# Another written order for the steady blocks, the opening and the last two blocks of a fused attention and feed-forward kernel, without the hold on batch 3's loads

## The chip, the cores and the metric

The kernel runs on one core of one Trainium2 chip. The metric is the device time of one execution in microseconds; the time before is the median of three runs.

## The reference

```
k_proj = einsum('ks,bhsd->bhkd', E, k);  v_proj = einsum('ks,bhsd->bhkd', F, v)
scores = matmul(q, k_proj^T) / sqrt(64)
attn = exp(scores - max);  attn = attn / (sum(attn) + 1e-09)
x = matmul(attn, v_proj)  -> transposed and reshaped to (8192, 512)
h = x @ w_in;  g = h * (1 / (1 + exp(-1.702 * h)));  out = g @ w_out
```

q, k and v are (8, 8, 1024, 64): 8 batches, 8 heads, 1024 positions, 64 wide. E and F are (64, 1024), w_in is (512, 2048), w_out is (2048, 512). All are float32 in DRAM; the kernel computes in bf16 with float32 sums.

## The kernel before, in words

**Blocks.** The 8192 rows are taken in 16 blocks of 512, numbered j = 0 to 15; batch b holds blocks 2b and 2b + 1. TensorE (PE) does all products; every product lands in one of eight PSUM banks, and VectorE (DVE) or ScalarE (ACT) must read it from there before the bank can be written anew.

**Batch work** (once for two blocks): `ld` loads k and v of the next batch, `lq` loads its q (both on GpSimd's, POOL's, DMA queue), `pj` projects k and v (16 matmuls of 128 rows by 64 columns), `kb` copies the projected k out of PSUM, `kd` and `qd` transpose k and q by DMA on SyncE's (SP's) queue, `vq` copies the projected v. `hold` is a copy of one element on POOL that waits for a transfer to land, so that what is queued behind it on POOL, `ld` and `lq`, starts no earlier. For j = 4 it reads the broadcast of block 3 (the tile rbc), for other blocks the transposed k and q of the batch (lines 723 to 726).

**Attention of a block:** `sc.0`, `sc.1` (scores: eight matmuls each of 64 rows by 32 columns, "small tiles"), `ex` (four exponentials on ACT, which need another activation table than the gelu; `gt` loads the gelu's table back), `su` (the sums of the exponentials, small tiles), `den` (copies of them), `ga` (a DMA that spreads them over 128 partitions), `rc` (reciprocal on DVE), `sr` (a DMA to DRAM), `sb` (two DMAs that broadcast them to all partitions as rbc), `va.0`, `va.1` (attention times v, small tiles) and `mv` (four products with rbc on DVE that give xT, the input of the feed-forward part). For block 3 the DMAs ga, sr and sb go on POOL's queue, otherwise on SP's. In blocks 0 to 2 the tokens are normalised in another way (`tk`, `tm`, `xr`, `xc`).

**Feed-forward part.** Both products are done with seven instead of eight half-size products (Winograd's form of Strassen's scheme). First product: for each of four column groups n the steps `un.P1` to `un.P7` (four matmuls of 128 by 128 by 256 each) add up in three accumulators A, B and G in three banks; `un.c1`, `c2`, `c3` copy, `d1`, `d2` add, and `g11`, `g12`, `g21`, `g22` are the gelus on ACT that write gT. `xs` and `gs` are the sums of inputs that the scheme needs (DVE). Second product: `F1` to `F7`, each in two halves of eight such matmuls; `Fc1` to `Fc3` copy, `Fd1`, `Fd2` add, `Fo0`, `Fo1` copy to the output tile, `st` stores. The temporaries of block 2's first groups lie in the buffer that rbc uses (line 622).

**Order.** Nothing is scheduled by a planner at run time: each engine executes its instructions in the order in which they are written, and the order is three lists of words. `OPEN` (line 480) is run once, from F1.0 of block 1 to block 5; `STEPS` (line 465) is run for j = 5 to 13, where `u2.c1` means block j, `va.0+1` block j + 1 and `st0-1` block j - 1, and the batch words are left out for odd j (lines 834 to 839); `END` (line 524) is run last, for blocks 13 to 15. In `OPEN` and `END` a word is step@block, `!` moves a copy to the other engine, and the numbers behind the colon are the PSUM banks; in `STEPS` the banks come from `BANK` (line 476) and the engine of a copy from `ON_ACT`. A step that writes a bank waits until the last reader of what stood there is done. Text below writes sc.0@2 for the step sc.0 of block 2.

In the list before, PE's small-tile steps of a steady block stand in four places: `va.0`, then `va.1` and (even j) `pj`, then `sc.0 sc.1`, then `su`, with full 128 by 128 matmuls between them.

Of the kernel before, what the change touches and what calls it, by code (L numbers as in the profile page):

```python
# [18 lines left out]
def kernel(ctx, tc, q, k, v, E, F,  # L19
                                                     moe_w_in, moe_w_out, out):  # L20
    nc = tc.nc
    B, H, S, D = q.shape
# [3 lines left out]
    J = S // P  # L26
# [430 lines left out]
    def ffn2_ops(j):  # L457
# [23 lines left out]
        F1.0@1:0 F1.1@1 sc.0@2:1,2 Fc1@1!:3 sc.1@2:4,5 ex.0.1@2 ex.0.0@2 F5.0@1:6 ex.1.1@2 F2.0@1 F6.0@1
        tk.0.1@2:7 tm.0.1@2 tk.1.0@2:2 tk.0.0@2:1 tm.0.0@2 F6.1@1 ex.1.0@2 tk.1.1@2:5 tm.1.0@2 Fc2@1! F2.1@1
        tk.2.1@2:4 tm.1.1@2 xr.0.0@2:7 xr.0.1@2:1 Fo0@1 xr.1.0@2:2 F5.1@1 tm.2.1@2 xr.1.1@2:5 xc.1.0@2
        tk.3.1@2:0 xc.1.1@2 tk.3.0@2:4 xc.0.1@2 F7.0@1 xc.0.0@2 sc.1@3:2,5 sc.0@3:1,7 ex.1.0@3 tm.3.0@2 ex.1.1@3
        F7.1@1 Fc3@1! ex.0.0@3 xr.3.0@2:4 tk.2.0@2:2 Fd1@1 tm.3.1@2 ex.0.1@3 F3.0@1 su@3:5,1 xc.3.0@2 den.0@3
        den.1@3 tm.2.0@2 xs.0@2 xr.2.1@2:7 u0.P1@2:0 u0.c1@2:5 xc.2.1@2 F4.0@1 xr.3.1@2:4 F4.1@1 xc.3.1@2
        xr.2.0@2:1 qd@4 xs.1@2 xc.2.0@2 u1.P1@2:2 Fo1@1 u0.P5@2:7 u0.P6@2 u1.c1@2:3 u1.P6@2 u0.P2@2 u0.c3@2!
        u1.P5@2:4 u1.c2@2 xs.2@2 u0.c2@2! u1.c3@2! u0.P3@2 pj@4:1 u0.d2@2 gt@2 u0.g11@2 u1.P3@2 u1.P7@2 ga@3
        kb@4! u0.P7@2 rc@3 u1.d2@2 u2.P1@2:7 u1.d1@2 u1.P2@2 u0.d1@2 u3.P5@2:0 xs.3@2 u0.g12@2 u1.g12@2
        u2.P5@2:4 u1.g22@2 u0.g22@2 u0.P4@2 vq.1@4 u1.P4@2 F3.1@1 gs1.0@2 u2.c3@2! Fd2@1 u1.g11@2 sr@3 kd@4  # L490
        u0.g21@2 u2.c1@2:2 u3.P1@2:5 u3.c3@2 u1.g21@2 st0@1 st1@1 u2.P2@2 u2.P6@2 u2.P3@2 u3.c1@2:6 u3.P2@2
        u3.P6@2 u2.g11@2 sc.0@4:3,7 vq.0@4 u3.g11@2 u2.c2@2! sc.0@5:1,5 u2.P7@2 u3.c2@2 u2.d2@2 ex.0.1@4
        ex.0.1@5 u2.d1@2 u3.P3@2 u3.P7@2 sb@3 u2.P4@2 ex.0.0@5 u3.d2@2 va.0@3:4,7 ex.0.0@4 u3.d1@2 sc.1@5:0,5
        mv.0.0@3 ex.1.1@5 ex.1.0@5 u3.P4@2 sc.1@4:1,3 mv.0.1@3 va.1@3:4,5 F1.0@2:7 ex.1.1@4 su@5:0,3 ex.1.0@4
        mv.1.0@3 su@4:4,1 mv.1.1@3 F1.1@2 xs.0@3 den.1@4 den.0@4 den.0@5 xs.2@3 u1.P1@3:5 xs.1@3 gt@2 u2.g21@2
        u0.P5@3:1 u3.g21@2 Fc1@2:2 u2.g12@2 ga@4 u0.P1@3:4 den.1@5 u1.P5@3:6 u0.c1@3:0 F2.0@2 u0.P2@3 u0.P6@3
        u3.g22@2 u1.c3@3! F2.1@2 u1.c1@3:3 u1.P6@3 u3.g12@2 u1.P2@3 u2.g22@2 gs2.0@2 gs3.0@2 u1.P3@3 gs1.1@2
        u1.c2@3 u0.c3@3 gs2.1@2 u0.g11@3 u3.P1@3:4 rc@4 u1.d2@3 u1.P7@3 F6.0@2 u0.P3@3 F6.1@2 F5.0@2:6 Fc2@2
        Fo0@2 F5.1@2 u2.P1@3:7 u0.c2@3 gs3.1@2 u1.g11@3 F7.0@2 sr@4 xs.3@3 F7.1@2 Fc3@2! u0.d2@3 u3.c1@3:5 Fd1@2
        ga@5 u3.P6@3 u0.P7@3 u1.g12@3 u1.d1@3 u3.P2@3 F4.0@2 F4.1@2 u0.d1@3 gs4.1@2 u2.c1@3:1 u2.P6@3 sb@4  # L500
        u0.P4@3 u3.c2@3 Fo1@2 u0.g12@3 gs4.0@2 u1.g22@3 u0.g21@3 u3.P5@3:2 F3.0@2 u2.c2@3! u3.c3@3! u0.g22@3
        rc@5 gs3.0@3 hold@4 ld@4 u3.P7@3 F3.1@2 Fd2@2 u3.P3@3 u1.P4@3 u1.g21@3 u3.d2@3 u2.P2@3 va.0@4:0,6 u2.g11@3
        pj@6:2 gs1.0@3 u3.g11@3 sr@5 u3.d1@3 u3.g22@3 vq.0@6 va.1@4:3,7 u2.P5@3:4 u2.P7@3 u2.c3@3 kb@6! u3.P4@3
        mv.0.1@4 lq@4 mv.1.1@4 mv.0.0@4 xs.0@4 F1.0@3:6 u2.d1@3 vq.1@6! u2.P3@3 u0.P5@4:7 u3.g21@3 mv.1.0@4
# [42 lines left out]
    def step(name, j, banks=None, swap=False):  # L547
# [324 lines left out]
```

## Time and profile before

| | us |
|---|---|
| median of 3 runs | 474.62 (474.2 to 475.11) |
| the profiled execution | 474.2, of which its span 472.4 |
| PE busy | 462.0 |
| VectorE busy | 331.8 |
| ScalarE busy | 319.1 |
| GpSimd busy | 92.7 |
| block 6 (with pj) / block 7 (without), from list start to list start | 28.30 / 26.46 |

The span is the time from the program's first instruction to its last in the profiled execution. Busy time is the union of an engine's instructions; matmuls are pipelined, so PE's rate is read from the distance between starts, not from durations. In the profile's lines "L639" is line 639 of the kernel (the P steps), L585 the F steps, L274 the small tiles of sc and va, L701 su and L184 the projection. A chain of waits is followed back from the last instruction, at each step to what released it.

| DMA of the profile | queue | issues | median us to landing |
|---|---|---|---|
| k of a batch | POOL | 7 | 11.3 |
| v of a batch | POOL | 7 | 14.8 |
| q, an eighth of a batch | POOL | 48 | 16.2 |
| rbc from DRAM (sb) | SP | 24 | 7.3 |
| stores | SP | 31 | 2.7 |

### The profile page before, as it was taken

What the parts mean: (1) busy time and instruction counts of PE and PEld (TensorE: products, weight loads), DVE (VectorE), ACT (ScalarE), POOL (GpSimd) and SP (SyncE); (2) the same over time, 40 slices, a digit from 0 to 9 for tenths busy, and PEclk for the clock granted to TensorE, in tenths of its full rate; (3) what the DMA queues carried; (4) which work ended last, traced back from release to release, by engine and by line L of the source; (5) the groups of instructions that cost most, each with busy time, mean ns of one, the idle gap of its engine ahead of it and who ended that gap; (6) DMA issues with size and microseconds to landing.
All of it is one profiled execution on the core that took longest, in us unless ns stands there. A gap on an engine that the chain in (4) does not pass through costs nothing.

```text
span 472.4 us, 10651 instructions
## 1 busy us (share of the span) xinstructions
PE 462.0 (98%) x4378; PEld 361.1 (76%) x4378; DVE 331.8 (70%) x626; ACT 319.1 (68%) x557; POOL 92.7 (20%) x116
## 2 busy tenths in 40 slices
PE   8999999999989999999999999999999999999996
PEld 4644447768778778887878788787888878888885
DVE  4586896778774875858687685868768585859472
ACT  2665464696456977868686786957687796758461
POOL 7562161134006002402061020610100000000000
PEclk9999999999999999999999999999999999999999
DMA  9999999979989919993699909999391414512022
GB/s 170 200 188 206 230 168 146 180 184 188 181 199 207 216 37 242 178 180 99 123 201 195 203 8 179 213 195 140 77 194 31 103 51 93 162 20 90 1 90 89
DMA packets 132863, 69.20 MB, mean 146 GB/s; under 512 B 98236, under 2 KB 122316, under 8 KB 132816
## 3 DMA queue, kind: packets, MB, share of 16 engines
q0 software_dynamic: 86848, 30.45, 58.8%
q1 hardware_dynamic: 45888, 37.82, 33.4%
q8 instruction: 34, 0.56, 0.5%
q10 hardware_dynamic: 80, 0.26, 0.2%
q14 instruction: 13, 0.11, 0.1%
HBM read 72.88 MB, written 16.99 MB: 190 GB/s over the span
## 4 chain that ended last, share of the span: by engine, by line
PE 71%; DMA 22%; DVE 2%; ACT 1%; POOL 1%; SPq 1%; issue 1%; DVEq 0%; POOLq 0%
PE k_ps L585 34%; PE k_ps L639 31%; DMA v_sb<-in_v_dram 5%; DMA q_sb<-in_q_dram 4%; DMA rbc<-rdr 4%; PE k_ps L274 3%; DMA w_in_sb<-in_moe_w_in_dram 2%; DMA w_out_sb<-in_moe_w_out_dram 2%; PE k_ps L184 2%; DMA kt<-k_b 2%; DMA rc<-o_sb 2%; DMA rdr<-rc 1%; PE k_ps L701 1%; DVE xT L675 1%; SPq L264 1%
## 5 line engine op out<-in xcount | busy, mean ns | idle before, releaser
L570 DVE TENSOR_TENSOR q_even<-k_ps,q_even 128x512 f32<-128x512 f32 x108 | 72.5, 686 | 47.3 <-PE k_ps L639 45.8
L585 PEld LDWEIGHTS <-sg 128*128 128x128 bf16 x960 | 93.4, 98 | 12.5 <-issue 1.4
L639 PEld LDWEIGHTS <-late 128*128 128x128 bf16 x896 | 86.6, 98 | 13.5 <-PE k_ps L585 1.8
L639 PE MATMUL k_ps<-xw,late 128*128 128x256 bf16 x672 | 95.2, 273 | 0.3 <-DVE xw L447 0.3
L585 PE MATMUL k_ps<-tw,sg 128*128 128x256 bf16 x720 | 88.9, 273 | 0.2 <-DVE q_even L570 0.2
L655 ACT ACTIVATE gT<-k_ps 128x512 bf16<-128x512 f32 x112 | 66.6, 599 | 22.2 <-PE k_ps L639 20.7
L585 PEld LDWEIGHTS <-gT 128*128 128x128 bf16 x720 | 70.2, 98 | 10.4 <-issue 2.1
L639 PEld LDWEIGHTS <-w_in_sb 128*128 128x128 bf16 x672 | 63.1, 98 | 17.4 <-issue 10.2
L655 ACT ACTIVATE gT<-q_even 128x512 bf16<-128x512 f32 x108 | 64.3, 629 | 12.1 <-DVE q_even L570 11.8
L639 PE MATMUL k_ps<-xT,w_in_sb 128*128 128x256 bf16 x448 | 66.9, 273 | 0.3 <-ACT k_ps L643 0.3
L585 PE MATMUL k_ps<-w_out_sb,gT 128*128 128x256 bf16 x480 | 59.9, 273 | 1.3 <-DVE xT L675 1.3
L567 ACT COPY q_even<-k_ps 128x512 f32<-128x512 f32 x61 | 34.9, 590 | 32.2 <-PE k_ps L639 32.0
L71 POOL DMA_DIRECT2D q_sb<-in_q_dram x48 | 42.1, 904 | 56.9 <-DMA v_sb<-in_v_dram 27.7
L455 DVE TENSOR_TENSOR sg<-gT 128x1024 bf16<-128x1024 bf16 (+2 forms) x62 | 41.0, 662 | 0.4 <-ACT gT L655 0.4
L675 DVE TENSOR_TENSOR xT<-k_ps,rbc 128x512 bf16<-128x512 f32 x52 | 33.5, 680 | 7.3 <-DMA rbc<-rdr 3.8
L567 DVE COPY q_even<-k_ps 128x512 f32<-128x512 f32 x47 | 31.4, 685 | 10.0 <-PE k_ps L639 9.2
L643 ACT COPY k_ps<-k_ps 128x512 f32<-128x512 f32 x56 | 31.9, 588 | 8.8 <-PE k_ps L639 3.6
L570 DVE TENSOR_TENSOR o_sb<-k_ps,u_sb 128x512 f32<-128x512 f32 (+1 forms) x31 | 20.9, 674 | 21.7 <-PE k_ps L585 21.6
L639 PE MATMUL k_ps<-xw,w_in_sb 128*128 128x256 bf16 x224 | 33.4, 273 | 0.0
L639 PE MATMUL k_ps<-xT,late 128*128 128x256 bf16 x224 | 33.3, 273 | 0.0
L667 ACT ACTIVATE expT<-k_ps 128x512 bf16<-128x512 f32 x56 | 29.2, 606 | 5.7 <-PE k_ps L274 5.5
L585 PE MATMUL k_ps<-tw,gT 128*128 128x256 bf16 x240 | 30.2, 273 | 0.0
(131 smaller groups left out, 523.8 us busy)
## 6 DMA issues: line engine op xcount, KB each, us to landing
out_dram<-o_sb SPq DMA_DIRECT2D x31, 512.0 KB, 2.7
rbc<-rdr SPq DMA_DIRECT2D x24, 512.0 KB, 7.3
k_sb<-in_k_dram POOLq DMA_DIRECT2D x7, 1024.0 KB, 11.3
v_sb<-in_v_dram POOLq DMA_DIRECT2D x7, 1024.0 KB, 14.8
q_sb<-in_q_dram POOLq DMA_DIRECT2D x48, 128.0 KB, 16.2
w_in_sb<-in_moe_w_in_dram POOLq DMA_DIRECT2D x8, 256.0 KB, 11.1
w_out_sb<-in_moe_w_out_dram POOLq DMA_DIRECT2D x4, 512.0 KB, 11.5
q_even<-in_q_dram POOLq DMA_DIRECT2D x12, 128.0 KB, 15.1
```

The costliest lines, as they stand in the source:

```text
L71: nc.gpsimd.dma_start(out=qt[b][:, j], in_=qv[:, j])
L184: nc.tensor.matmul(kvps[b][r], eft(j, slice(e * KP, (e + 1) * KP)), (kt, vt)[e][b][:, :, j, :], start=(j == 0), stop=(j == J - 1))
L274: nc.tensor.matmul(outs[i][r.start + c:r.start + c + w], lhsTs[i][ri, c:c + w], rhss[i][ri], start=True, stop=True)
L455: nc.vector.tensor_tensor(t[i - 1], in0, in1, op=ALU.add if i == 1 else ALU.subtract)
L567: (nc.scalar.copy if (n in ON_ACT) != swap else nc.vector.tensor_copy)(out_, in_)
L570: nc.vector.tensor_tensor(out_, in0, in1, op=ALU.add)
L585: nc.tensor.matmul(at_(n)[:, 0 if one else t], x[:, c, t * P:(t + 1) * P], w[:, c], start=(i in (1, 5) and (one or t == 0) and c == 0), st ...
L639: nc.tensor.matmul(at_(h)[:, r], a[:, c, f:f + P], w[:, c], start=(i in (1, 5) and r == 0 and c == 0), stop=(i in (2, 3, 4) and r == 1 and ...
L643: nc.scalar.copy(new(f"B{m}", [P, 2, TH], f"B{n}"), at_(f"A{n}"))
L655: nc.scalar.activation(out_, in_, AF.Gelu_apprx_sigmoid)
L667: nc.scalar.activation(expT[j][:, 2 * u + t, :], at_(f"S{u}{t}"), AF.Exp, scale=scale)
L675: nc.vector.tensor_tensor(x_of(j)[:, u, :], at_(f"V{p[1]}{t}"), rbc[j][:, u, :], op=ALU.mult)
```

## The change

The three lists, the banks of the steady list and the set of copies that ACT does are replaced, and `hold` no longer has a case for j = 4; the new OPEN has no word hold@4 (and has one more `gt`, for block 4). Every other step of the lists is there exactly once as before, with the same operands. In the new STEPS the small tiles stand in three places: `va.1 va.0`, then `sc.1` (`pj`) `sc.0`, then `su`. `kb` goes from DVE to ACT, `c3` of group 3 from ACT to DVE. The diff, with OPEN and END cut to lines that the text speaks of:

```diff
     STEPS = """
-        F3.0-1 u2.c1 Fo1-1 u0.d2 rc+2 F3.1-1 u2.P5 u3.c3 u3.P7 u0.g22 Fd2-1 u2.P6 u0.g12 u2.c2 u2.c3 u2.P2
-        u2.g11 u3.P3 va.0+1 u3.d1 st0-1 gs1.0 u3.P2 u3.d2 u3.g11 u2.P3 u3.g12 mv.0.1+1 u2.P7 va.1+1 pj+4 u3.g22
-        u3.P4 u2.d2 st1-1 u2.g12 u3.g21 u2.d1 mv.0.0+1 kb+4 F1.0 mv.1.0+1 u2.g22 vq.0+4 u2.P4 mv.1.1+1 gs1.1
-        u2.g21 vq.1+4 F1.1 u0.P1+1 sr+2 sc.0+3 gs2.0 gs2.1 sc.1+3 Fc1 ex.0.0+3 gs3.0 u1.P1+1 xs.0+1 ex.1.1+3
-        xs.2+1 gs3.1 F2.0 F2.1 ex.1.0+3 xs.1+1 kd+4 ex.0.1+3 F6.0 F6.1 Fc2 u0.c1+1 su+3 u1.c1+1 u0.P6+1 den.0+3
-        u0.P2+1 Fo0 den.1+3 gs4.1 u1.P6+1 F7.0 u1.P2+1 u1.P5+1 u0.c2+1 F5.0 u1.c2+1 gt u0.g11+1 u1.c3+1 F5.1
-        ga+3 Fc3 u1.P7+1 F7.1 u1.g11+1 xs.3+1 gs4.0 u1.P3+1 u2.P1+1 u0.P5+1 u1.d1+1 u3.P1+1 Fd1 u0.c3+1 u1.P4+1
-        F4.0 u0.P7+1 sb+2 u1.d2+1 u0.d1+1 qd+4 hold+4 ld+4 lq+4 u1.g21+1 u3.c1+1 F4.1 u1.g12+1 u3.P6+1 u3.c2+1
-        u0.P4+1 u1.g22+1 u3.P5+1 u0.P3+1 u0.g21+1
+        u2.c3 Fd2-1 u3.P2 u3.d1 u3.P3 u2.d1 u3.d2 u3.g11 u2.g22 u2.P3 u3.P4 va.1+1 ga+2 u3.g21 u3.g22 u2.d2
+        u3.g12 st1-1 va.0+1 u2.P4 u2.g21 mv.1.1+1 F1.0 F1.1 mv.0.1+1 u2.g12 mv.0.0+1 sc.1+3 mv.1.0+1 gs1.1
+        xs.0+1 pj+4 rc+2 Fc1 ex.1.0+3 sc.0+3 st0-1 u0.P1+1 gs2.1 F2.0 kb+4 gs2.0 ex.0.1+3 vq.1+4 vq.0+4 xs.1+1
+        F2.1 gs4.1 ex.0.0+3 ex.1.1+3 gs3.0 sr+2 F5.0 F6.0 Fo0 u1.P5+1 xs.3+1 u0.c1+1 F6.1 u1.P1+1 F5.1 u1.c3+1
+        gs3.1 Fc2 F7.0 u0.P6+1 u1.c1+1 kd+4 u0.P5+1 u1.P6+1 xs.2+1 u0.c2+1 Fc3 u1.P3+1 u0.P2+1 F7.1 u1.P2+1
+        u0.c3+1 sb+2 qd+4 hold+4 ld+4 lq+4 u1.c2+1 gt u0.g11+1 u1.P7+1 gs4.0 u0.P7+1 u1.g11+1 u0.P3+1 Fd1
+        u1.d1+1 F4.0 u3.P1+1 u1.P4+1 u0.d2+1 F4.1 u0.g12+1 u1.g21+1 u1.d2+1 u1.g22+1 su+3 u1.g12+1 u0.d1+1
+        u0.P4+1 den.1+3 u3.c1+1 u2.P1+1 den.0+3 u0.g22+1 F3.0 u3.P5+1 u0.g21+1 u3.c3+1 u3.P6+1 F3.1 u2.c1+1
+        gs1.0+1 Fo1 u2.P6+1 u2.P2+1 u3.c2+1 u2.c2+1 u2.P5+1 u2.g11+1 u3.P7+1 u2.P7+1
     """.split()
-    BANK = dict(FD=0, FB=4, FG=0, A0=6, A1=1, B0=7, B1=3, G0=2, G1=5, S10=5, S11=7, V00=4, V01=0, S00=3, S01=2,
-                V10=6, V11=5, D0=2, D1=5, PJ=1)
-    ON_ACT = ('Fc1', 'Fc3', 'c2.2', 'c3.0', 'c3.1', 'c3.2', 'c3.3', 'vq')
+    BANK = dict(FD=0, FB=1, FG=2, A0=3, A1=6, B0=5, B1=0, G0=4, G1=7, S10=4, S11=5, V00=6, V01=7, S00=6, S01=7,
+                V10=3, V11=2, D0=4, D1=7, PJ=2)
+    ON_ACT = ('Fc1', 'Fc3', 'c2.2', 'c3.0', 'c3.1', 'c3.2', 'kb', 'vq')

     OPEN = """
-        F1.0@1:0 F1.1@1 sc.0@2:1,2 Fc1@1!:3 sc.1@2:4,5 ex.0.1@2 ex.0.0@2 F5.0@1:6 ex.1.1@2 F2.0@1 F6.0@1
...
-        u1.P5@2:4 u1.c2@2 xs.2@2 u0.c2@2! u1.c3@2! u0.P3@2 pj@4:1 u0.d2@2 gt@2 u0.g11@2 u1.P3@2 u1.P7@2 ga@3
...
-        u3.g22@2 u1.c3@3! F2.1@2 u1.c1@3:3 u1.P6@3 u3.g12@2 u1.P2@3 u2.g22@2 gs2.0@2 gs3.0@2 u1.P3@3 gs1.1@2
-        u1.c2@3 u0.c3@3 gs2.1@2 u0.g11@3 u3.P1@3:4 rc@4 u1.d2@3 u1.P7@3 F6.0@2 u0.P3@3 F6.1@2 F5.0@2:6 Fc2@2
...
-        rc@5 gs3.0@3 hold@4 ld@4 u3.P7@3 F3.1@2 Fd2@2 u3.P3@3 u1.P4@3 u1.g21@3 u3.d2@3 u2.P2@3 va.0@4:0,6 u2.g11@3
...
+        F1.0@1:0 F1.1@1 Fc1@1:1 F5.0@1:2 sc.0@2:3,4 sc.1@2:5,6 F2.0@1 ex.0.1@2 F6.0@1 ex.0.0@2 F2.1@1 tk.1.0@2:7
...
+        u1.c2@2! ga@3 xr.2.0@2:6 u1.d2@2 xc.2.0@2 u0.P3@2 pj@4:5 u0.c2@2 gt@2 u1.g12@2 u0.P7@2 u0.d2@2 rc@3
...
+        sc.1@5:3,6 u3.P3@2 u1.g21@2 u2.P7@2 u0.g21@2 ex.1.0@5 u3.d1@2 ex.1.1@5 sb@3 u2.c3@2! u3.d2@2 sc.0@5:2,1
+        u2.d1@2 ld@4 u3.P4@2 st0@1 u2.P3@2 sc.1@4:4,3 u2.P4@2 ex.0.0@5 ex.0.1@5 ex.1.1@4 u2.d2@2 su@5:6,2
+        ex.1.0@4 sc.0@4:7,1 st1@1 ex.0.0@4 va.0@3:3,4 F1.0@2:7 den.1@5 F1.1@2 mv.0.1@3 mv.0.0@3 ex.0.1@4
...
+        u0.c2@3! F5.0@2:2 Fo0@2 u2.P1@3:7 u1.c2@3 u0.d2@3 rc@4 u2.c1@3:5 sr@4 rc@5 F6.0@2 gs3.1@2 u1.g11@3
+        xs.2@3 F6.1@2 u2.P2@3 F5.1@2 u1.P5@3:3 Fc2@2 u2.g11@3 u0.g12@3 F7.0@2 xs.3@3 F7.1@2 u0.P7@3 u1.c3@3
...
     END = """
...
-        u3.g21@15 u2.g21@15 Fc2@15 F7.0@15 gs4.1@15 F7.1@15 F2.0@15 Fc3.0@15 Fd1@15 F2.1@15 F4.0@15 F4.1@15
-        Fo0@15 F3.0@15 Fd2.0@15 F3.1@15 Fd2.1@15 Fo1@15 sp.0@15 sp.1@15 sp.2@15 sp.3@15
...
+        F2.1@15 Fc3.1@15 gs4.1@15 Fc3.0@15 Fd1@15 F4.0@15 F4.1@15 F3.1@15 Fd2.1@15 Fo0@15 sp.0@15 F3.0@15
+        Fd2.0@15 Fo1@15 sp.1@15 sp.3@15 sp.2@15
     """.split()
@@ def step
         elif i == "hold":
-            for n, src in enumerate((rbc[3][:1, 0, :1], rbc[3][D:D + 1, 0, :1]) if j == 4 else
-                                    (kts[b % 2][:1, 0, :1], qT[b][:1, J - 1, 0, :1])):
-                nc.gpsimd.tensor_copy(held[:, n:n + 1], src)
+            nc.gpsimd.tensor_copy(held[:, :1], kts[b % 2][:1, 0, :1])
+            nc.gpsimd.tensor_copy(held[:, 1:], qT[b][:1, J - 1, 0, :1])
```

## The prediction

> **What bounds the kernel now.** I read the page first, then PE's timeline over two middle blocks, then the chain that ended last in blocks 2 to 4, then PE's timeline there.
>
> ```profile
> PE 462.0 (98%) x4378; PEld 361.1 (76%) x4378; DVE 331.8 (70%) x626; ACT 319.1 (68%) x557; POOL 92.7 (20%) x116
> PE   8999999999989999999999999999999999999996
> PEclk9999999999999999999999999999999999999999
> ```
>
> PE is busy in all slices at a full granted clock; VectorE and ScalarE have 30% to spare. So only two things can be saved: moments in which PE changes shape, and waits too short to show in tenths. PE's timeline in blocks 7 and 8:
>
> ```profile
> 240.77 0.60 PE L639 MATMUL k_ps<-xT,late 128*128 128x256 bf16 x4
> 241.30 0.41 PE L274 MATMUL k_ps<-expT,vq 64*32 64x512 bf16 x8
> 241.64 0.61 PE L639 MATMUL k_ps<-xT,w_in_sb 128*128 128x256 bf16 x4
> ...
> 246.03 0.60 PE L639 MATMUL k_ps<-xT,w_in_sb 128*128 128x256 bf16 x4
> 246.56 0.63 PE L274 MATMUL k_ps<-qT,kt 64*32 64x512 bf16 x16
> 247.11 0.61 PE L639 MATMUL k_ps<-xT,w_in_sb 128*128 128x256 bf16 x4
> ```
>
> Four full matmuls run from one start to the next in 0.437 us (0.109 each). 241.64 - 240.77 - 0.437 = 0.433 goes to one group of eight small tiles, 247.11 - 246.03 - 0.437 = 0.643 to two together; the first full matmul after a burst is 0.01 late on top. So a group costs 0.21 and each burst 0.23 besides (0.09 on entry, 0.14 on leaving). With these prices the timeline of blocks 5 to 13 adds up with no wait at all: two blocks take 54.75 us (216.94 to 271.70), 448 full matmuls and their small ones. Waits stand in the opening only:
>
> ```profile
> 76.09 13.03 DMA v_sb<-in_v_dram
> 89.12 0.04 issue
> 89.16 1.89 PE k_ps L184 x15
> ...
> 95.48 7.28 DMA rbc<-rdr
> ...
> 107.20 7.55 DMA rc<-o_sb
> ...
> 115.16 5.41 DMA rdr<-rc
> ...
> 121.42 10.40 DMA rbc<-rdr
> ```
>
> ```profile
> 127.61 0.41 PE L274 MATMUL k_ps<-expT,vq 64*32 64x512 bf16 x8
> ...
> 129.79 0.41 PE L274 MATMUL k_ps<-expT,vq 64*32 64x512 bf16 x8
> 130.14 1.05 PE L639 MATMUL k_ps<-xw,late 128*128 128x256 bf16 x8
> 131.02 0.60 PE L639 MATMUL k_ps<-xw,w_in_sb 128*128 128x256 bf16 x4
> 132.69 1.03 PE L585 MATMUL k_ps<-w_out_sb,gT 128*128 128x256 bf16 x8 [1.07 <-DVE xT L675]
> ```
>
> The chain runs through transfers: batch 2's v lands at 89.12, then the denominators of block 4 go out (7.55), back to DRAM (5.41), and as a broadcast to all partitions (10.40). It lands at 131.82; PE stops until VectorE's products (xT) are there.
>
> Counting every start on PE against the prices above: list work fills 393.45 us from 68.46 on, PE's last matmul starts at 468.37 and ends its slot at 468.48, so 6.57 us are waits. 1.0 is before sc.0@2 (kt<-k_b lands at 71.3), 1.17 before pj@4 (v), and 4.34 come after it: 1.7 between 97 and 104 (eight exponentials in a row on ScalarE, then the broadcast of block 3), 0.36 at 115, 2.1 from 131 to 138, 0.2 in bits.
>
> **Part 1, bursts in the steady list.** Block without a projection: va.0 | va.1 | sc.0 sc.1 | su are four bursts, then three: 0.23 saved. Block with one: va.0 | va.1 pj | sc sc | su become va va | sc.1 pj sc.0 | su. The last fence prices the sandwich: u2.P2 begins at 127.08, so va, pj and va take 130.14 - 127.08 - 0.44 = 2.62; va with pj alone takes 216.94 - (214.75 - 0.09) = 2.28 (PE's timeline, block 6). Before: 0.44 + 2.29 + 0.65 + 0.44 = 3.82; after: 0.65 + 2.63 + 0.44 = 3.72; saved 0.10. The loop has five of the first kind (5, 7, 9, 11, 12), three of the second (6, 8, 10), and block 13 has only va (0.23): 5 x 0.23 + 3 x 0.10 + 0.23 = **1.7 us**. In OPEN the number of bursts (15) and of shape changes within them (3) is the same in both lists, in END too.
>
> The count alone, nine blocks at 0.23, would say 2.1. The Trainium skill, "TensorEngine Tiling (Array Packing)", Key Properties, says that changing the tiling mode, not the tile, drains TensorE: by it the projection inside the scores pays two changes of its own. The fence above has their price (127.61 to the first pair of pj at 127.95 is 0.34, not 0.21), so I keep 1.7.
>
> **Part 2, what PE does before 89.12.** The landing of v comes from POOL's queue and is not moved. Before pj@4 the old list has 13 F steps and 8 P steps of full matmuls, the new one 14 and 8: one F step more (8 x 0.109 = **0.87 us**) is done while v is on its way. That F step is F5.0@1 ahead of sc.0@2, which shortens the wait for kt from 1.0 to 0.15; the new list then has 0.9 for xc.2.0@2 before u0.P3@2, hidden by the wait for v. After pj@4 remain 374.95 us of PE work before and 372.36 after: 2.59 = 1.72 + 0.87.
>
> **Part 3, waits after pj@4.** I laid the new list end to end on each engine from rows: an operation begins 0.37 us after the start of the matmul it waits for, takes 0.60 on ScalarE or 0.69 on VectorE (0.49 to 0.61 from start to start), a matmul follows 0.07 after it (mv ends 132.62, F1.0 starts 132.69).
> - Steady blocks. The tightest handovers: u3.P3, u3.d2, va.0 on bank 7: PE has 0.11 + 0.87 + 0.09 + 0.21 = 1.29 in between, the chain needs 0.30 + 0.07 + 0.69 + 0.07 = 1.13. F1.1, Fc1, F2.0 on bank 0 and u3.P4, u3.g21, F1.0: 1.21 against 1.03. All hold, by 0.16 to 0.18; the old list's tightest hold by 0.29. In block 13, without scores, F2.0 comes 0.55 after F1.1: 0.48 lost. (The old list gave that handover 0.98 there and lost nothing.)
> - rc now follows its ga sooner: with batch loads running ga takes 7.0 (253.24 to 260.26) or 7.55, without them 2.0. The steady list leaves 8.0 between them and 1.5 more before F6.0: hidden.
> - Blocks 2 and 3: c1 on bank 5 before u3.P6@2 0.5; exponentials before su@5 and va.0@3 and F1.0@2 1.2; bits 0.5.
> - Block 4's chain: ga@4 goes out at 108.7, with batch 3's loads (now from 95.9 to 124) beside it, so rc@4, then rc@5, stand on VectorE until 116 to 117; behind them wait gs3.1, xs.2 and Fc2@2, and F7.0@2 waits for Fc2: **1.8 us**, a new wait. With 2.0 instead of 7.55 it would be none. From there sr 5.4, and sb@4 when the loads have ended (6.9 to 7.3): it lands by 130, va.0@4 is at 130.9. The 2.1 us from 131 on go.
> - Removing hold: sb@3 goes out at 94.7 as before (it waits for block 2's temporaries in the same buffer), ld@4 at 95.9 instead of 103.76, behind it on POOL's queue, and lq@4 behind that; nothing else waits in that queue until hold@6. If sb@3 keeps 7.28 it lands at 102.7, the products are due at 103.8: covered by 1.1.
>
> Sum 0.5 + 1.2 + 0.5 + 1.8 + 0.2 + 0.5 (block 13) = 4.7. The same laying-out of the old list gives 3.2 where its trace has 4.34, so I add 0.5: 5.2. At best (ga 2.0, no shortfall) 2.9; at worst 8.
>
> No change is made behind PE: the last add, its store and the rest of the span (468.48 to 472.4) stay; SP sends the last block's four stores in an order that fits the new F3.1, F3.0. END, laid out so, has no wait. The copies that change engines (kb to ScalarE, c3.3 to VectorE) lie beside PE, which covers them as long as the handovers above hold.
>
> **Sum.** PE ends at 89.19 + 372.36 + 5.2 = 466.75 against 89.19 + 374.95 + 4.34 = 468.48: -1.7 us. The profiled execution took 474.2 (span 472.4), the median of three 474.62, 0.4 above; so 474.62 - 1.7 = **472.9 us**.
>
> **Rivals.** Within 0.2% (0.95 us) is no change.
> - *The opening's waits mostly vanish*: ga@4 takes 2.0, nothing falls short: after-pj waits 2.9, PE ends 4.0 earlier: 470.6. For it: the loads start 8 us earlier, so block 4's chain may meet their thin end. Against: ga took 7.0 even 13 us into a load.
> - *The steady list does not hold*: 0.16 us of slack is used up by any later VectorE operation; 0.15 in each of nine blocks is 1.35, leaving -0.35: 474.3, no change. For it: slacks half of the old list's. Against: laid out so, the old list's VectorE starts agree with its trace within 0.06 us.
> - *The broadcast of block 3 is stretched by the loads that hold kept back* (slower). It is on the chain: every us beyond 8.4 stops PE. At 10.40 (the row of sb@4, beside loads) it costs 2.0 and eats the gain; at 14.3, what v takes beside k and q, 5.9. It decides from 10.1 on; at 12.5 the time is 477.
>
> The Trainium skill, "DMA: Bandwidth & Descriptors", Queues, rings and completion order, says that each DMA engine takes turns between queue rows, packet by packet. By it SP's transfers (ga, sr, sb@4) share with POOL's loads, which speaks against taking hold out, while sb@3, ahead of ld@4 in POOL's own ring, is not stretched: the sum stays -1.7; by the 10.40 row it is +0.3. The trace of before has no broadcast with loads behind it on one queue, so it can't decide.
>
> **How the numbers follow.** Forecast (471.9 to 473.9) 0.50, vanishing waits 0.18, steady list not holding 0.19, stretched broadcast 0.13. A tenth of the forecast's share lies within 0.95 of no change (about what a measurement of this kernel can tell). Of the list that does not hold, 0.02 is still faster, 0.16 no change, 0.01 slower. Faster 0.45 + 0.18 + 0.02 = 0.65; same 0.05 + 0.16 = 0.21; slower 0.13 + 0.01 = 0.14. Range 470.5 (best case) to 475.6 (the broadcast at 11 or so).
>
> **What would show it.** Right: block pairs of 54.4 us with no waits on PE, three bursts per block; pj@4 at 89.1 again; ld@4 near 96; a VectorE wait at rc@4 near 114 to 117 and PE's at F7.0@2. Wrong: small repeated gaps at va.0, F1.0 or F2.0 in every block; rbc<-rdr of block 3 landing after 104; v landing at another time than 89.

## The result, and the profile after

| | before | after |
|---|---|---|
| median, us | 474.41 (474.02 to 475.11, 4 runs) | 470.53 (470.08 to 471.2, 4 runs) |
| ratio | | 0.9918, 95% interval 0.9901 to 0.9935 |
| profiled execution / its span | 474.2 / 472.4 | 470.48 / 468.7 |
| v of batch 2 lands / PE goes on | 89.12 / 89.16 | 89.10 / 89.14 |
| two blocks, with and without pj | 54.75 | 54.42 (28.19 + 26.22) |
| block 13 | 25.35 | 25.55 |
| PE work behind that v (by starts) | 374.95 | 372.36 |
| waits of PE behind that v | 4.34 | 3.25 |
| slot of PE's last matmul ends | 468.48 | 464.78 |

Faster, by 3.9 us, where 1.7 was forecast; the time is 0.03 above the lower edge of the range. "PE work" counts the matmuls at the prediction's prices, and the waits are what is left of the time from v to PE's end. One run each of E8 (479.09 us) and E12 (482.01 us) below, slower than the rest at a lower granted clock, is left out of their medians. From the page of the changed kernel, first the busy times, then the shares of the chain that ended last (before: PE 71%, DMA 22%):

```profile
PE 460.4 (98%) x4378; PEld 361.4 (77%) x4378; DVE 332.1 (71%) x625; ACT 322.1 (69%) x560; POOL 86.1 (18%) x114
PE 82%; DMA 12%; POOL 3%; DVE 2%; ACT 1%; issue 1%; POOLq 0%; DVEq 0%
```

PE has the same number of matmuls, VectorE is as busy as it was and ScalarE 3.0 us more: no operation became cheaper. PE loses less to changes of shape and stands less. PE's timeline of the changed kernel in block 6 (start, duration, engine, line, operation, tiles, shape, count):

```profile
212.09 0.62 PE L274 MATMUL k_ps<-expT,vq 64*32 64x512 bf16 x16
...
214.93 0.41 PE L274 MATMUL k_ps<-qT,kt 64*32 64x512 bf16 x8
215.27 0.40 PE L184 MATMUL k_ps<-k_sb,eft 128*64 128x512 bf16 x1
...
217.12 0.41 PE L274 MATMUL k_ps<-qT,kt 64*32 64x512 bf16 x8
217.46 0.61 PE L639 MATMUL k_ps<-xT,w_in_sb 128*128 128x256 bf16 x4
```

Both groups of va are one burst, the projection stands between the groups of scores, and no idle time is noted at any of these lines. From the first score to the first full matmul it is 217.46 - 214.93 = 2.53; with the 0.09 of entry and the 0.01 by which the first full matmul is late that is the 2.63 that the prediction counted.

The chain of the changed kernel between 60 and 140 us:

```profile
76.12 12.97 DMA v_sb<-in_v_dram
89.10 0.04 issue
89.14 1.90 PE k_ps L184 x15
...
100.76 14.95 DMA q_sb<-in_q_dram
115.71 0.35 DVE rc L712
116.06 0.55 DVE sg L455
116.60 0.33 DVE xw L447
116.93 0.61 DVE u_sb L567
...
117.58 1.91 PE k_ps L585 x16
```

The first three lines are those of before within 0.06 us. Of the small transfers of blocks 4 and 5 only one still matters to the chain: VectorE stands at rc@5 until 115.70, Fc2 (u_sb) comes behind it, and F7.0@2 on PE behind that. The broadcast of block 4 that landed at 131.82 is gone from the chain; its first half now lands at 124.6, va.0@4 starts at 129.46, and from 118 to block 13 PE has no wait above 0.15.

The chain names a transfer of q as what released rc, while what rc@5 reads is the transfer ga@5; the two end near each other (q at 115.71, ga@5 at 115.61). VectorE's timeline there:

```profile
114.02 0.35 DVE L712 RECIPROCAL rc<-rc 128x32 f32<-128x32 f32 x1 [0.59 <-DMA rc<-o_sb]
...
115.70 0.35 DVE L712 RECIPROCAL rc<-rc 128x32 f32<-128x32 f32 x1 [1.33 <-DMA q_sb<-in_q_dram]
...
116.85 0.68 DVE L567 COPY u_sb<-k_ps 128x512 f32<-128x512 f32 x1
```

It is the second reciprocal, rc@5, that costs: 1.33 us of standing, and Fc2 is 1.15 behind it. On PE:

```profile
117.58 1.91 PE L585 MATMUL k_ps<-tw,sg 128*128 128x256 bf16 x16 [0.75 <-DVE u_sb L567]
```

The step ahead of it, four matmuls, starts at 116.23; so by starts the wait before F7.0@2 is 117.58 - 116.23 - 0.437 = 0.91. The bracket, which goes by modelled ends, says 0.75. PE's waits go by starts below, except in brackets.

### The profile page after: what moved, and what is told of

It is laid out like the page before. It is cut to its first block, busy times and chain, and to the rows that moved or that the text cites. A ratio compares the mean times of both kernels' runs of the same rounds, so it can differ in the third digit from the quotient of the medians.

```text
span 468.7 us, 10645 instructions
## 1 busy us (share of the span) xinstructions
PE 460.4 (98%) x4378; PEld 361.4 (77%) x4378; DVE 332.1 (71%) x625; ACT 322.1 (69%) x560; POOL 86.1 (18%) x114
## 4 chain that ended last, share of the span: by engine, by line
PE 82%; DMA 12%; POOL 3%; DVE 2%; ACT 1%; issue 1%; POOLq 0%; DVEq 0%
PE k_ps L585 35%; PE k_ps L639 33%; DMA v_sb<-in_v_dram 5%; PE k_ps L367 4%; DMA q_sb<-in_q_dram 3%; DMA q_even<-in_q_dram 3%; PE k_ps L379 3%; PE k_ps L184 3%; PE k_ps L274 3%; POOL k_sb L59 1%; PE k_ps L701 1%; POOL v_sb L59 1%; POOL q_sb L71 1%; DVE xT L675 1%; DVE q_even L570 0%
## 5 line engine op out<-in xcount | busy, mean ns | idle before, releaser
L585 PEld LDWEIGHTS <-sg 128*128 128x128 bf16 x960 | 93.5, 98 | 12.5 <-issue 1.6
L639 PE MATMUL k_ps<-xw,late 128*128 128x256 bf16 x672 | 89.1, 273 | 0.4 <-ACT k_ps L643 0.4
L655 ACT ACTIVATE gT<-k_ps 128x512 bf16<-128x512 f32 x112 | 65.5, 596 | 22.0 <-PE k_ps L639 17.2
L570 DVE TENSOR_TENSOR q_even<-k_ps,q_even 128x512 f32<-128x512 f32 x108 | 70.5, 685 | 11.9 <-PE k_ps L639 9.8
L585 PE MATMUL k_ps<-w_out_sb,gT 128*128 128x256 bf16 x480 | 58.6, 273 | 0.1
L567 DVE COPY q_even<-k_ps 128x512 f32<-128x512 f32 x50 | 34.3, 688 | 28.4 <-PE k_ps L639 17.3
L567 ACT COPY q_even<-k_ps 128x512 f32<-128x512 f32 x58 | 33.8, 588 | 23.7 <-PE k_ps L639 23.4
L639 PE MATMUL k_ps<-xT,late 128*128 128x256 bf16 x224 | 31.8, 273 | 0.0
L585 PE MATMUL k_ps<-w_out_sb,sg 128*128 128x256 bf16 x240 | 31.0, 273 | 0.0
## 6 DMA issues: line engine op xcount, KB each, us to landing
k_sb<-in_k_dram POOLq DMA_DIRECT2D x7, 1024.0 KB, 12.3
```

What stands on the lines that cost most here:

```text
L567: (nc.scalar.copy if (n in ON_ACT) != swap else nc.vector.tensor_copy)(out_, in_)
L570: nc.vector.tensor_tensor(out_, in0, in1, op=ALU.add)
L585: nc.tensor.matmul(at_(n)[:, 0 if one else t], x[:, c, t * P:(t + 1) * P], w[:, c], start=(i in (1, 5) and (one or t == 0) and c == 0), st ...
L639: nc.tensor.matmul(at_(h)[:, r], a[:, c, f:f + P], w[:, c], start=(i in (1, 5) and r == 0 and c == 0), stop=(i in (2, 3, 4) and r == 1 and ...
L655: nc.scalar.activation(out_, in_, AF.Gelu_apprx_sigmoid)
```

## The experiments

Steps and banks that a diff doesn't show are those of the changed kernel, or of the kernel before where it says so. Each ratio is to runs of the kernel before that were taken together with the experiment.

| | median, us (runs) | ratio to before, 95% interval |
|---|---|---|
| the changed kernel | 470.53 (4) | 0.9918, 0.9901 to 0.9935 |
| E1 four bursts per block | 472.87 (12) | 0.9966, 0.9953 to 0.9979 |
| E2 projection last in its burst | 470.44 (6) | 0.9911, 0.989 to 0.9932 |
| E3 new lists, hold kept | 475.27 (12) | 1.0023, 1.0 to 1.0047 |
| E4 old lists, no hold | 472.32 (9) | 0.995, 0.9929 to 0.9971 |
| E5 rc@5 behind Fc2@2 | 469.87 (6) | 0.9916, 0.99 to 0.9932 |
| E6 two P steps behind pj@4 | 473.5 (12) | 0.9988, 0.9971 to 1.0005 |
| E7 block 13 in another order | 470.45 (6) | 0.9921, 0.9904 to 0.9938 |
| E8 hold kept, rc@5 behind Fc2@2 | 472.26 (9) | 0.9961, 0.9938 to 0.9985 |
| E9 E2, E5 and E7 together | 469.45 (6) | 0.9907, 0.9888 to 0.9926 |
| E10 one P step ahead of pj@4 | 470.56 (6) | 0.9936, 0.9914 to 0.9959 |
| E11 E10 and a copy earlier | 470.71 (6) | 0.9934, 0.9916 to 0.9951 |
| E12 sb@3 on SP's queue | 475.28 (9) | 1.0022, 1.0009 to 1.0035 |

### E1: what a burst costs

```diff
-        u3.g12 st1-1 va.0+1 u2.P4 u2.g21 ...
+        u3.g12 st1-1 u2.P4 va.0+1 u2.g21 ...
```

> The new kernel with u2.P4 put between va.1 and va.0 in the steady list, so that each block has four bursts again. If a burst costs 0.23 us wherever it stands, blocks 6 to 14 lose 9 x 0.23 = 2.1 us against the new kernel (profiled span 468.7 to 470.8, time 470.5 to 472.6), and each pair of steady blocks takes 54.87 instead of 54.42. The rival, that the count of bursts is hidden behind waits of VectorE and ScalarE and the gain lies in the opening alone, gives 470.5 again and 54.42 a pair.

Measured: 472.87, 2.3 above the changed kernel. Every block of the loop is 0.23 longer (26.45, 28.42, and 25.78 for block 13), nine times 0.23 = 2.07; the rest, 0.3, lies in the opening, which this edit doesn't touch. So the price of a burst is what the prediction read from before's timeline, and with the burst back an odd block is as long as before (26.45); the even blocks keep 0.12 and block 13 keeps 0.43 above before.

### E2: the projection inside the scores

```diff
-        xs.0+1 pj+4 rc+2 Fc1 ex.1.0+3 sc.0+3 st0-1 ...
+        xs.0+1 rc+2 Fc1 ex.1.0+3 sc.0+3 pj+4 st0-1 ...
```

> The new kernel with the projection behind both scores (sc.1 sc.0 pj) instead of between them: one change of shape less in each of blocks 6, 8 and 10. By the prices of shape changes 0.126 us each, 0.38 in all: 470.1 and a pair of 54.29. If only entering and leaving full-size work costs, and a change between two small shapes is free, nothing moves (54.42).

PE's timeline of E2 in block 6:

```profile
215.20 0.62 PE L274 MATMUL k_ps<-qT,kt 64*32 64x512 bf16 x16
215.76 0.40 PE L184 MATMUL k_ps<-k_sb,eft 128*64 128x512 bf16 x1
...
217.61 0.61 PE L639 MATMUL k_ps<-xT,w_in_sb 128*128 128x256 bf16 x4
```

From the first score to the first full matmul it is 217.61 - 215.20 = 2.41, against 217.46 - 214.93 = 2.53 with the projection inside: 0.12 for the second change between the two kinds of small tile. Blocks 6, 8 and 10 take 28.07. The Trainium skill's rule that a change of the tiling mode drains PE ("TensorEngine Tiling (Array Packing)", Key Properties) agrees, and the trace has its price here, 0.12 us. The median shows only 0.1 of the 0.36, because the opening of the profiled execution took 0.3 more: F7.0@2 stood 1.07, and va.1@3 another 0.2.

### E3 and E4: each part alone

E3 has the new lists, with the word hold@4 ahead of ld@4 and the old code of `hold`. E4 has the old lists without the word hold@4:

```diff
E3
-        u2.d1@2 ld@4 u3.P4@2 ...
+        u2.d1@2 hold@4 ld@4 u3.P4@2 ...
E4 (the kernel before)
-        rc@5 gs3.0@3 hold@4 ld@4 u3.P7@3 ...
+        rc@5 gs3.0@3 ld@4 u3.P7@3 ...
```

> The new lists with hold@4 put back ahead of ld@4, so batch 3's loads start near 104.5 instead of 96.4 and end near 131 instead of 120.5. If the loads beside block 4's chain were what stopped PE from 131 on in the old kernel, sb@4 (out at about 119.5) takes about 10 again, lands near 130 and PE waits 0.5 to 1.5 us at block 4: 471 to 472. The rival, that most of the gain comes from removing the hold, gives 473 or more. A third view, that the hold protects the broadcast of block 3 (landing at 103.9 in the new kernel against 102.8), gives a gain of about 1 us from it: 469.5.

> The old lists with the one word hold@4 taken out. Loads of batch 3 then start near 96 and end near 121. The waits of 2.1 us from 131 on depend on sb@4 (out at 121.4, landed at 131.8 beside the loads); without loads it takes 5 to 7 and lands by 128.5, so those waits fall to 0 to 0.5, while ga@4 and sr@4 stay as slow and block 3's broadcast may land 1 us later and cost up to 1: 472.4 to 473.8. If the hold does nothing for the time: 474.4. If it is the whole gain: 470.7.

E4: 472.32, 2.1 below before. Its ld@4 goes out at 96.34, and the opening (from F1.0@1 to block 5) takes 111.89 instead of 114.06 us: the three waits from 131 on (2.1 together) are gone, as in the changed kernel. The 0.36 at 115 is gone too, and the wait before va.1@3, behind block 3's products, is 0.3 longer. Where PE had stood 1.07 in before (131.02 to 132.69 in the prediction's lines), E4 goes from 131.38 to 131.82, four matmuls without a wait. So taking out hold is worth 2.1 by itself, and the lists 1.8 on top of it.

E3: 475.27, where I expected 471 to 472; the rival was right. Without the other part the new lists are not 1.8 faster than before but a little slower, or the same. VectorE's timeline of E3 where the changed kernel's was shown:

```profile
115.10 0.35 DVE L712 RECIPROCAL rc<-rc 128x32 f32<-128x32 f32 x1 [2.43 <-DMA rc<-o_sb]
...
118.06 0.35 DVE L712 RECIPROCAL rc<-rc 128x32 f32<-128x32 f32 x1 [2.61 <-DMA rc<-den]
...
119.20 0.68 DVE L567 COPY u_sb<-k_ps 128x512 f32<-128x512 f32 x1
```

With the loads from 103.27 on instead of 96.4, ga@4 takes 7.5 us (107.54 to 115.07) and ga@5 9.5 (108.47 to 117.97), and VectorE stands in front of both reciprocals. PE waits 4.0 before F7.0@2 (the four matmuls ahead of it start at 115.48), and the steps behind it lose another 1.7. First PE's timeline of E3, then the row of its page with the clock that TensorE was granted, in 40 slices of 11.8 us:

```profile
119.94 2.28 PE L585 MATMUL k_ps<-tw,sg 128*128 128x256 bf16 x15 [3.87 <-DVE u_sb L567]
```

```profile
PEclk9999999999899999999999999999999999999999
```

The 1.7 is no wait but the clock. The 28 full matmuls from 119.94 take 4.72 us to the next step at 124.66, where they take 3.06 at the full rate, and read microsecond by microsecond the granted clock is 0.50 from 121.1 to 124.5; in the changed kernel it is 1.00 up to the last matmuls. Of E3's twelve runs one has a mean granted clock of 0.999 and took 473.71; the others have 0.989 to 0.996 and took 474.41 to 480.35. In E8 below, where the stand is gone, the nine runs have 0.998 to 1.000. That the stand of PE brings the clock down fits all of this, but was not tried apart.

The old list could bear such a ga, since there rc@5 stands 18 steps of PE behind rc@4; the new one has both reciprocals ahead of Fc2@2. As the lists are written, the two parts of the change are no sum of two terms: the new ones need loads that start early.

### E5 and E8: the reciprocal ahead of Fc2

```diff
-        ... sr@4 rc@5 F6.0@2 gs3.1@2 ...
+        ... sr@4 F6.0@2 gs3.1@2 ...
-        ... u1.P5@3:3 Fc2@2 u2.g11@3 ...
+        ... u1.P5@3:3 Fc2@2 rc@5 u2.g11@3 ...
```

E8 has the same edit in E3, so with hold.

> The new kernel with one word moved: rc@5, the reciprocal of block 5, stands behind Fc2@2 on VectorE instead of right behind rc@4. In the new kernel PE waits 0.91 us before F7.0@2, and VectorE stands at rc@5 until 115.70. If that reciprocal is what F7.0@2 waits for, Fc2@2 ends by about 116 and the wait goes: 0.9 less, 469.6. If rc@4 (landed 113.99) is the one, or the banks, nothing moves: 470.5.

> The new lists with hold@4 kept, and rc@5 behind Fc2@2. With hold kept the new lists took 475.3, and PE waited 4.0 us before F7.0@2 and 1.7 in the steps after it, while VectorE stood at rc@4 until 115.10 and at rc@5 until 118.06. If the hold's price in the new lists is that stand at rc@5, moving it gives back 3 to 4.5 us: 471 to 472.3. If the price is the transfers' lateness in itself (block 4's broadcast), less than 1 comes back: 474.5.

E5: 469.87, 0.7 below the changed kernel; F7.0@2 starts without a wait (116.88, four matmuls after 116.45) and the opening takes 114.36 instead of 115.05. E8: 472.26, 3.0 below E3. Hold costs 4.7 in the new lists as they are, and 2.4 with rc@5 behind Fc2@2 (472.26 against 469.87), about what it costs in the old lists. So about half of the 4.7 comes from one word, rc@5, standing on VectorE ahead of Fc2@2, and from the halved clock behind that stand. With the word moved the two parts of the change nearly add up: the lists with hold are 1.9 below the 474.14 of before that was taken with E8 (0.7 to 2.9 by the interval), and taking out hold gives 2.4 more.

### E6, E10 and E11: does PE work ahead of v save its length?

The prediction's second part books 0.87 us for one step more that is done while v is on its way. E6 moves two steps back behind pj@4, E10 moves one more ahead of it, and E11 lets ScalarE free a bank earlier besides.

```diff
E6
-        u0.c1@2:1 u1.P3@2 xs.2@2 ... xr.2.0@2:6 u1.d2@2 xc.2.0@2 u0.P3@2 pj@4:5 u0.c2@2 ...
+        u0.c1@2:1 xs.2@2 ... xr.2.0@2:6 xc.2.0@2 pj@4:5 u0.P3@2 u1.P3@2 u1.d2@2 u0.c2@2 ...
E10
-        ... xc.2.0@2 u0.P3@2 pj@4:5 ... u2.c1@2:0 u1.P7@2 u1.g11@2 ...
+        ... xc.2.0@2 u1.P7@2 u0.P3@2 pj@4:5 ... u2.c1@2:0 u1.g11@2 ...
E11, besides E10
-        ... u2.g11@2 u3.c1@2:5 u0.P2@2 ...
+        ... u3.c1@2:5 u2.g11@2 u0.P2@2 ...
```

> The new kernel with u0.P3@2 and u1.P3@2 (8 full matmuls, 0.87 us) put behind pj@4 instead of ahead of it. If v's landing at 89.1 pins PE there, PE waits 0.87 more at pj@4 and the work behind it is 0.87 longer: 471.4, with pj@4's first v matmul at 89.1 again. If what counts is only the sum of the work, and waits behind pj@4 shrink by as much, 470.5.

> The changed kernel with one step of full matmuls, u1.P7 of block 2 (0.437 us), moved from behind the projection of batch 2 to ahead of it, where PE waits 0.59 us for v. The prediction's second part, taken literally (each step done while v is on its way is time saved): 0.44 less, 470.1 us, the wait ahead of the projection 0.15. Rival (behind the projection ScalarE is the bound: it works from the copy of the projected k at 91.1 to the last of eight exponentials at 103.9 with hardly a gap, and PE waits for it at u3.P6 of block 2 and at F1.0 of block 2): the wait before u3.P6 of block 2 grows from 0.54 to 0.98 and the time stays at 470.5.

> As the kernel with u1.P7 of block 2 ahead of the projection, and ScalarE's copy u3.c1 of block 2 ahead of its gelu u2.g11, so that u3.P6 of block 2 can start 0.5 us earlier. Theory of single handovers: the wait before u3.P6 is 0.5 again and 0.44 is won: 470.1 us. Rival (ScalarE's whole queue up to the last exponential bounds the stretch, so the order inside it is worth nothing): the wait moves on to F1.0 of block 2, which starts at 103.5 as before, and the time stays at 470.5.

E6: 473.5, 3.0 above the changed kernel, so neither theory. PE's timeline of E6 behind the projection:

```profile
91.36 1.05 PE L639 MATMUL k_ps<-xT,late 128*128 128x256 bf16 x8
93.85 0.60 PE L639 MATMUL k_ps<-xw,late 128*128 128x256 bf16 x4 [1.45 <-DVE rbc L567]
```

The two steps took 0.87, and then PE stood for u0.P7: VectorE, in the order of the list, had been waiting since 89.85 for the adds of the moved steps, and the copy that u0.P7 needs was behind them. Also, PE stood 1.25 for kt at sc.0@2 in this execution, where the changed kernel does not stand, so that it was at pj only at 89.45 and the projection ended 0.4 later. 0.87 + 1.6 + 0.4 = 2.9. The edit moved VectorE's work too, and so is no clean test of the 0.87.

E10 is: nothing on VectorE or ScalarE waits soon for u1.P7. PE reaches pj@4 at 89.06, as intended, and the time is 470.56 instead of the 470.1 that the prediction's rule gives. First the line of PE's timeline in the changed kernel where PE stands again behind v, then that of E10:

```profile
95.44 0.60 PE L639 MATMUL k_ps<-xw,late 128*128 128x256 bf16 x4 [0.38 <-ACT k_ps L643]
```

```profile
95.42 0.60 PE L639 MATMUL k_ps<-xw,late 128*128 128x256 bf16 x4 [0.39 <-ACT k_ps L643]
```

This is u3.P6@2, and it starts at the same time in both, since ScalarE's copy of its accumulator comes from a queue that begins with the projected k at 91.06. The 0.44 that PE had won was lost already at u2.P6@2, which waits 0.43 for another copy of that queue. The exponentials start at 99.87 (99.89) and F1.0@2 at 103.45 (103.47).

E11 has no wait before u3.P6@2, but a new one of 0.27 before u3.P7@2, and the same 0.65 before F1.0@2. In its execution the projection ended 0.56 later than in E10, and F1.0@2 came 12.3 us behind that end, in E10 and in the changed kernel 12.5: at most 0.2 of the 0.44 is won, and the median, 470.71, shows nothing of it. The medians alone cannot tell 0.44 from nothing (the runs of one kernel lie up to 2 us apart); the traces can. Both times the rival was right about the time, though in E10 the new wait stands at u2.P6@2 and not at u3.P6@2 as it had said: from the landing of v to 103.5 ScalarE's queue is the bound, and the PE work moved ahead of v in E10 and E11 becomes a wait, wholly or for the most part.

### E7 and E9: the two waits of block 13, and a version that beats both

In E7 block 13 alone runs u1.P1+1 ahead of u0.P1+1, so that four more matmuls stand between F1.1 and F2.0. E9 has the edits of E2, E5 and E7.

```diff
-    for j in range(5, 14):
-        for word in STEPS:
+    at13 = list(STEPS)
+    at13.remove("u1.P1+1")
+    at13.insert(at13.index("u0.P1+1"), "u1.P1+1")
+    for j in range(5, 14):
+        for word in at13 if j == 13 else STEPS:
```

> The new kernel with u1.P1+1 ahead of u0.P1+1 in block 13 alone, where the scores are missing between F1.1 and F2.0. There PE waits 0.30 before u0.P1 (bank 3, mv.1.0) and 0.14 before F2.0 (bank 0, Fc1). With 0.44 us of full matmuls between, both should go: 0.4 less, 470.1, and block 13 takes 25.1 instead of 25.55 in the trace. If bank 6 (mv.0.0) or xT comes late too, the wait only moves.

> The changed kernel with three edits that were tried singly: the projection at the end of the burst of scores, rc of block 5 behind Fc2 of block 2, and in block 13 u1.P1+1 ahead of u0.P1+1. Theory (the three prices stand in three places that do not touch: shape changes in blocks 6, 8 and 10, the wait at F7.0 of block 2, the two waits of block 13): even blocks 28.07, block 13 25.25, no wait at F7.0 of block 2, so 0.36 + 0.9 + 0.3 = 1.6 less: about 469.0 us. Rival (what is won in the opening is lost again at the next handover, as the gains of the single trials of 0.1 and 0.6 by the medians hint): 469.7 to 470.2.

PE's timeline in block 13, of the changed kernel and then of E7:

```profile
402.56 1.91 PE L585 MATMUL k_ps<-w_out_sb,gT 128*128 128x256 bf16 x16
404.60 0.61 PE L639 MATMUL k_ps<-xT,w_in_sb 128*128 128x256 bf16 x4
```

```profile
401.84 1.91 PE L585 MATMUL k_ps<-w_out_sb,gT 128*128 128x256 bf16 x16
403.59 1.04 PE L639 MATMUL k_ps<-xT,w_in_sb 128*128 128x256 bf16 x8
```

Sixteen full matmuls are 1.75 from the first start to the next; the changed kernel's next step comes after 2.04, E7's after 1.75. Both waits there, 0.30 and 0.14, are gone, and 0.14 comes back before F7.0. Block 13 takes 25.25 instead of 25.55; the median, 470.45, is too near to tell it apart.

E9: 469.45 (469.08 to 469.94), the fastest of all; its runs lie below all those of the changed kernel, by 1.1 in the median, where the sum of the three prices is 1.6: between the theory (469.0) and the rival (469.7 to 470.2). In its trace all three are there (28.07, 25.25, no wait at F7.0@2). What came back is in the opening: the second half of block 3's broadcast took 8.84 and landed at 104.69, VectorE stood 1.32 for it, and the burst that ends with va.1@3 lost 0.53 instead of 0.12. Also, the projection of batch 2 ended 0.3 later in this execution.

### E12: block 3's broadcast on the other queue

```diff
-                queue.dma_start(out=rbc[j][r], in_=rdr[j][None, :, e, :].to_broadcast([D, HP, TB]))
+                nc.sync.dma_start(out=rbc[j][r], in_=rdr[j][None, :, e, :].to_broadcast([D, HP, TB]))
```

> The changed kernel with the broadcast of block 3 issued on SP's queue instead of POOL's; as POOL then waits for nothing there, the loads of batch 3 start some 3 us earlier (about 93) and run beside the broadcast instead of behind it. My theory (the place behind the broadcast in one queue is what keeps it short: 6.7 and 8.4 us to landing in the changed kernel's trace, against 10.40 for a broadcast beside loads in the trace of before): the second half lands after 104.5, PE waits 0.5 to 2.5 us more between 103 and 106, 471.0 to 473 us. [...] Rival (the queue makes no difference, all transfers share the same engines): it lands by 104 as before, and the time stays at 470.5 or gains a little from the earlier loads.

Measured: 475.28, 4.8 above the changed kernel. VectorE's timeline, first of the changed kernel, then of E12:

```profile
104.01 1.29 DVE L675 TENSOR_TENSOR xT<-k_ps,rbc 128x512 bf16<-128x512 f32 x2 [0.86 <-DMA rbc<-rdr]
```

```profile
106.72 1.29 DVE L675 TENSOR_TENSOR xT<-k_ps,rbc 128x512 bf16<-128x512 f32 x2 [2.90 <-DMA rbc<-rdr]
...
110.79 0.69 DVE L706 COPY o_sb<-k_ps 128x512 f32<-128x512 f32 x1 [2.32 <-DMA out_dram<-o_sb]
```

The second half goes out at 95.49 and lands at 106.60, 11.1 us, where in POOL's queue, with the loads behind it, it took 8.4; PE waits 1.45 before va.1@3 and 0.7 behind its first half. Behind it on SP stood two stores of block 1, the second of which lands 13.8 us after its issue (5.4 in the changed kernel); the sums of block 4 use the buffer of the second (line 704), so VectorE stands again, and PE 2.1 before u0.P1@3. Then the granted clock is 0.50 from 111.4 to 114.8, and the 16 full matmuls from 111.53 take 3.35 us instead of 1.75: another 1.6. The transposition that brings kt, ahead of the broadcast on SP's queue, took 7.1 us instead of 2.3, and PE waits 0.6 for it before sc.1@5. My theory had the direction and the first wait, 0.5 to 2.5; the stores, the clock and kt it had not counted. As the loads started 4.8 us earlier too (91.60 against 96.38), the queue's share and that of the earlier start are not told apart.

## Why the prediction was right, and where it was not

- **Direction and mechanism: right.** The waits stand where the text put them: nothing in the steady blocks, 0.91 at F7.0@2 behind rc@5 and Fc2@2, 0.54 at u3.P6@2, 0.44 in block 13 (0.48 forecast), 0.14 left from 131 to 138.
- **Bursts, 1.7 us: right.** Pairs of 54.42, blocks of 26.22 and 28.19, and E1's 0.23 in each of nine blocks. E2 bears out that pj inside the scores costs 0.12.
- **The work behind v, 2.59: right as an account** (372.36 PE work, v at 89.10). As a reason it is not shown: E10 moves one more step ahead of v, and that step's length is not won, so being ahead of v is not enough; whether the 0.87 itself is won, no run tells (E6 is no clean test). The account could hold because the waits of ScalarE's queue behind v were a term of their own.
- **The steady list holds: right,** though its tightest handovers had 0.16 us to spare: no block from 5 to 12 has a wait.
- **Waits behind v, 5.2: the term that was mis-sized;** it was 3.25, and the difference, 1.95, is the whole miss (3.7 won at PE's end against 1.7). By part: F7.0@2 0.91 for 1.8; the exponentials 0.79 for 1.2; bits 0.57 for 0.7; block 13 0.44 for 0.48; c1 0.54 for 0.5; and the 0.5 that was added because the same laying-out had been 1.1 short on the old list, 0. The first of these rested on a ga of 7.0 to 7.55 taken from before; ga@4 took 5.7 (108.29 to 113.99) and ga@5 6.4 (109.23 to 115.61). In the changed kernel the loads had begun 11.9 us before ga@4, in E3, where the same list has 7.5 and 9.5, only 4.3. Steady blocks fit: the changed kernel's ga issued 1.9 and 2.2 us behind the loads' start (234.21, 288.62) took 8.75 and 9.45, the one issued 20.1 behind (206.02) 5.9, and those 28 or more behind 2.0 to 2.7. What within the DMA engines makes this difference was not tried apart. Nothing in the prediction gives the shorter ga; to that extent the larger gain is luck.
- **The first rival's number, not its mechanism.** 470.6 was its time; but ga was never 2.0 and F7.0@2 did wait. The time lies where it does because the forecast's own waits were smaller, not because they vanished.
- **The third rival, the stretched broadcast: the mechanism exists, and came near.** Block 3's broadcast was to cost PE from a landing time of 8.4 on. In the changed kernel it took 6.7 and 8.4, in E9 8.84 with 0.4 lost, on SP's queue 11.1 with 2.2 of waits right behind it. The Trainium skill, "DMA: Bandwidth & Descriptors", Queues, rings and completion order, says that a DMA engine takes turns between queue rows; the prediction read from it that sb@3, ahead of the loads in their own ring, is not stretched. That is nearly so: its second half took 8.4 with the loads behind it and 7.5 in E3, where hold keeps them back, so 0.9 longer. On another queue than the loads (E12) it took 11.1, which agrees, within what is said there.

What none of the prediction's steps asked is whether its two parts are worth anything without each other. The new lists with hold are no faster than before (E3), hold's removal on the old lists gives 2.1 (E4), both together 3.9; with rc@5 behind Fc2@2 the lists give 1.9 even with hold (E8). Nor did it ask what a long stand of PE costs behind it: where PE stood 4.0 (E3) and 2.1 (E12), it then ran 3.4 us at half the granted clock.

## What to carry to other kernels

Before adding up the parts of a change to a written order, ask of each wait on an engine's queue (here a reciprocal behind a small DMA) how long that DMA takes under the traffic that the *other* part leaves, and what stands behind the waiting instruction: a 16 KB transfer of 5.7 to 9.5 us ahead of a copy that PE needs made one of the two largest swings in this study, 4.7 us, of which some 1.7 is the halved clock behind the stand. A step that PE does while it waits for a transfer is only worth its length if PE, and not the engine that reads the transfer's product, is the bound from there on. Bursts of small tiles could be priced from one timeline and counted; here that came out to within 0.1 us in every block.

## What the runs showed of the hardware that was not expected

- The same broadcast of block 3 (two halves) landed 6.7 and 8.4 us after its issue on POOL's queue with the loads behind it, and 11.1 (second half) on SP's queue with loads started before it; a store behind it on SP's queue took 13.8, where it takes 5.4 in the changed kernel and the median of the stores in that kernel's page is 2.8.
- A 16 KB transfer (ga) beside loads took 5.7 and 6.4 in the changed kernel, 7.5 and 9.5 in E3, where they had begun 7 us later; in the steady blocks of the changed kernel 8.75 and 9.45 with the loads 2 us old, and 2.0 once they are over.
- The clock granted to TensorE fell to 0.50 for 3.4 us in E3, 1.2 us into PE's work after a stand of 4.0, and in E12 at the end of a stand of 2.1 that had one of 1.45 two microseconds ahead of it. It cost 1.7 and 1.6 us. Behind a stand of 1.6 (E6, before u0.P7) it stayed at 1.00.
- Between executions of nearly the same opening, kt came later with nothing changed ahead of it: sc.0@2 starts at 71.68 in the changed kernel, 72.40 in E9 and 73.02 in E6. At the end of the projection 0.3 and 0.4 of this are left, since PE waits for v in between.
